# Moving 64 small SBUF copies of transposed e rows from GpSimd's queue to ScalarE's, with two row tiles in turn

## Chip, cores, metric

One core of one Trainium2 chip. The metric is the device time of one execution in microseconds (us). Most executions agree within 0.3%, some are up to 1% longer, so differences of a few us need several runs of both kernels on the same chip. PE is TensorE (PEld its weight loads), DVE is VectorE, ACT is ScalarE, POOL is GpSimd, SP is SyncE. A name with q (ACTq) is the engine's sequencer, which issues DMAs.

## The reference

The program computes a transformer block for one token (attention over a cache of 32 heads x 8192 rows x 192, then an MLP) and the gradients of its inputs, the large ones being dK and dV, each as large as its cache. The second half of the kernel forms them.

```
p = softmax(scores);  o = p @ v                        # scores = q @ k^T * Dh**-0.5
dV[j, :]  = p[j] * do                                  # outer product: one row of e times do
dS[j]     = p[j] * (V[j] . do - c);  dK[j, :] = dS[j] * q
```

## The kernel before

For each of 64 steps (half a head each) PE forms dV from `er_b`, a tile that holds rows of the transposed e at partitions 0, 32, 64 and 96. A row tile `er_t` is made once in four steps by a PE transpose and a ScalarE copy; `load_er` then moves 32 of its rows (8 KB) into `er_b` by a DMA. `load_er` and all stores are issued by GpSimd, whose instruction order the program doesn't pin. In the views, KB and VX are tiles in which dV and dK are formed and from which they are stored; VB takes V loads.

```python
ORDER = {mybir.EngineType.PE, mybir.EngineType.DVE, mybir.EngineType.Activation, mybir.EngineType.SP}
erp = ctx.enter_context(tc.tile_pool(name="erp", bufs=1))
...
def e_rows(t, pool=psS, tag="s"):
    ...                                            # PE transpose of E_all into ps
    er = erp.tile([P, P], BF16, name="er_t")
    A_.copy(out=er[0 : 2 * J, :], in_=ps[0 : 2 * J, :])
    return er
...
ctx.enter_context(tc.manual_schedule(engines=ORDER))
...
er_b = [bst.tile([P, R8, P], BF16, name=f"er_b{k}") for k in range(2)]
def load_er(s):
    er = er_b[s % 2]
    h, t = ht(s)
    r0 = (h % 2) * J + t * JH
    nc.gpsimd.dma_start(out=er[0:P:32, :, :], in_=er_t[0][r0 : r0 + JH, :])
    return er
...
V_.memset(er_b[1], 0.0)
er_l = {0: load_er(0), 1: load_er(1)}
...
def store(dst, s, src, lo=0, hi=JH):
    h, t = ht(s)
    nc.gpsimd.dma_start(out=dst[h][:, t * JH + lo : t * JH + hi, :], in_=src[:, lo:hi, :])
...
# weight gradients: two of the chunks are held back on purpose
keep = lambda w=cur["w"]: nc.gpsimd.dma_start(out=dst[:, :, lo : lo + CW], in_=w)
if dst is dwm_v and n in (GX - 2, GX - 1):
    kept.append(keep)
else:
    keep()
...
def dv_gen():
    for s in range(NS):
        dV, er, doh = out_b(2 * s), er_l.pop(s), do_of(ht(s)[0])
        for n, g in enumerate((0, 2, 4, 6, 1, 3, 5, 7)):
            dv_groups(dV, er, doh, (g,))           # PE matmuls with er, ScalarE copies into dV
            if n == 7:
                if s % 4 == 2 and s + 2 < NS:
                    er_t[0] = e_rows(TL - s // 4 - 1)
                if s + 2 < NS:
                    er_l[s + 2] = load_er(s + 2)
                store(dV_hd, s, dV, JQ if s == 0 else 0, JH)
...
# main loop, step s: dots on PE, dK on DVE, store of dK, next V load on SyncE
    if s in (NS - 4, NS - 3):
        kept.pop(0)()                              # the held-back stores go out in the last steps
```

Of the kernel before, what the change touches and what calls it, by code (L numbers as in the profile page):

```python
# [8 lines left out]
FP32 = mybir.dt.float32  # L9
# [11 lines left out]
def kernel(  # L21
# [26 lines left out]
    nc = tc.nc  # L48
    P = 128
    D = A_x.shape[-1]  # L50
    _, HQ, S, DH = A_k_cache.shape
# [4 lines left out]
    JH = J // 2  # L56
    JQ = J // 4
    TS = 16
    ND = D // P
# [13 lines left out]
    V_, A_, T_ = nc.vector, nc.scalar, nc.tensor  # L73
# [10 lines left out]

    dram = ctx.enter_context(tc.tile_pool(name="dram", bufs=1, space=bass.MemoryType.DRAM))
    ORDER = {mybir.EngineType.PE, mybir.EngineType.DVE, mybir.EngineType.Activation, mybir.EngineType.SP}
    erp = ctx.enter_context(tc.tile_pool(name="erp", bufs=1))

    A_.preload_act_table_set("natural_log_exp_and_others")
    ident_bf = const.tile([P, P], BF16, name="ident_bf")  # L90
# [63 lines left out]
    def layernorm(x, name):  # L154
        res = []
        for _ in g_layernorm(x, name, res):
            pass
        return res[0]
# [94 lines left out]
    n0, r0 = layernorm(x_c, "ln0")  # L253
# [83 lines left out]
    def e_rows(t, pool=psS, tag="s"):  # L337
        ps = pool.tile([P, P], BF16, name="er_ps", tag=tag)
        T_.transpose(out=ps[0 : 2 * J, :], in_=E_all[:, 2 * t : 2 * t + 2, :].rearrange("p h j -> p (h j)"), identity=ident_bf)
# [4 lines that stand above are left out]
    with tc.tile_pool(name="vs", bufs=3) as vsp, tc.tile_pool(name="ft", bufs=2) as ft, \  # L344
# [185 lines left out]
        if True:  # L530
# [224 lines left out]
            er_t = [e_rows(TL, psB, "b")]  # L755
# [8 lines left out]
    bst = ctx.enter_context(tc.tile_pool(name="bst", bufs=1))  # L764
# [83 lines left out]
    def load_er(s):  # L848

        er = er_b[s % 2]  # L850
        h, t = ht(s)
        r0 = (h % 2) * J + t * JH
        nc.gpsimd.dma_start(out=er[0:P:32, :, :], in_=er_t[0][r0 : r0 + JH, :])  # L853
        return er

    def ht(s):

        return H1 - s // 2, (1 - s % 2 if s < 4 else s % 2)
# [147 lines left out]
    nc.sync.dma_start(out=dao_bc, in_=dao_d.to_broadcast([P, D]))  # L1006
    V_.tensor_scalar(out=dx1, in0=e4, scalar1=vv[:, 0:1], scalar2=-1.0, op0=ALU.add, op1=ALU.mult)
    V_.tensor_tensor(out=dao, in0=dx1, in1=ga, op=ALU.mult)
    cpp, cp1 = bst.tile([P, DH], FP32, name="dq_junk")[:, 0 : HQ * ND].rearrange("p (h k) -> p h k", k=ND), bst.tile([P, HQ], FP32, name="cp1")
    V_.tensor_tensor(out=cpp, in0=AO.rearrange("p k h -> p h k"), in1=dao[:, None, :].to_broadcast([P, HQ, ND]), op=ALU.mult)  # L1010
    V_.reduce_sum(out=cp1, in_=cpp, axis=AX.X)
    V_.memset(er_b[1], 0.0)
    er_l = {0: load_er(0), 1: load_er(1)}
    dq_x = bst.tile([P, 12], FP32, name="dq_x")
    V_.memset(dha, 0.0)
# [268 lines left out]
# [4 lines that stand above are left out]
                dv_groups(dV, er, doh, (g,))  # L1288
# [6 lines that stand above are left out]
                elif n == 3 and s == 0:  # L1295
                    store(dV_hd, s, dV, 0, JQ)
                yield
# [26 lines left out]
    for s in range(NS):  # L1324
        h, t = ht(s)
# [3 lines left out]
        if s == 1:  # L1329
# [5 lines left out]
            out=dS4,  # L1335
# [77 lines left out]
```

## Time and profile before

| | before |
|---|---|
| time, median of 3 runs (range) | 1409.15 us (1407.72 to 1409.96) |
| bytes moved | 570.88 MB, mean 406 GB/s |
| DMA rate 700 to 1300 us | 416 GB/s, mean DMA share 1.01 |
| PE waits for er_b, ScalarE waits for er_t | 11.1 us, 10.5 us |

First the page's DMA queues (packets, MB, share of the 16 engines): q1 is SyncE's, q0 GpSimd's, q10 ScalarE's.

```profile
q1 hardware_dynamic: 55372, 342.48, 59.9%
q0 software_dynamic: 26736, 226.48, 38.8%
q10 hardware_dynamic: 20, 0.00, 0.0%
```

Then windows of the second half (start:end and length in us; busy us of PE, PEld, DVE, ACT and POOL; granted TensorE clock; DMA share, which is the busy share of the core's 16 DMA engines; GB/s). The first one is the start of the loop, where the transfers aren't saturated; after 586 us they are.

```profile
555.00:586.00 31.00, 26.98 (x393) 20.24 (x392) 26.49 (x75) 22.23 (x40) 12.08 (x20) 0.74 0.81 264
586.00:700.00 114.00, 83.25 (x752) 49.29 (x750) 79.96 (x107) 64.29 (x101) 19.38 (x33) 0.69 1.00 402
700.00:1300.00 600.00, 446.17 (x3664) 258.46 (x3662) 415.92 (x591) 356.09 (x519) 94.37 (x160) 0.65 1.01 416
```

Last, the timeline where the dV work begins (start, length, engine, line, idle before it in brackets). The move for this first step went out long before, at 555.7 us, and PE starts without a wait.

```profile
568.46 0.82 PE L1050 MATMUL dv_ps<-do_r,er_b 32*128 32x192 bf16 x8
568.57 0.17 ACT L1004 COPY h<-h_ps 128x5 f32<-128x5 f32 x1 [0.60 <-PE h_ps L907]
```

### The profile page before, as it was taken

The page shows a single profiled execution, that of the slowest core. Times are in us where ns is not written, and L with a number is a line of the kernel's source. Part 1 is how long each engine was busy: PE and PEld are TensorE (multiplying, and loading weights), DVE is VectorE, ACT ScalarE, POOL GpSimd, SP SyncE. Part 2 cuts the span into 40 slices and gives each one's busy share as a digit, 9 for nine tenths or more (in the row PEclk, how much of TensorE's full clock was granted, in tenths as well). Part 3 has the DMA queues.
Part 4 walks back from the last instruction along what each step waited for, and adds up shares of the span by engine and source line. Part 5 has one row for each costly group of instructions (what it writes and reads, how often), then busy time and mean ns, then how long its engine had stood idle before and what let it go on. Part 6 is the DMA issues. An engine that isn't in the chain of part 4 may idle for free. (4 is left out here: it accounts for less than half of the span.)

```text
span 1407.8 us, 30000 instructions
## 1 busy us (share of the span) xinstructions
PE 1121.3 (80%) x12543; PEld 745.1 (53%) x12543; DVE 1109.3 (79%) x1380; ACT 878.3 (62%) x1934; POOL 153.0 (11%) x270
## 2 busy tenths in 40 slices
PE   3999999899999998777867768787876777777783
PEld 1677777677777767444434434444443444444441
DVE  4999999999999998785767767676766766866783
ACT  0777777777777773655665656566654665655653
POOL 0000000000000001211111111111111111111111
PEclk9999999999999998876766675657576656665755
DMA  9999999999999998899999999999999999999998
GB/s 375 404 419 421 418 415 417 407 417 416 420 410 420 411 417 314 314 366 425 425 422 422 417 420 426 420 415 402 423 419 408 387 417 417 426 418 403 394 382 348
DMA packets 82264, 570.88 MB, mean 406 GB/s; under 512 B 12464, under 2 KB 31232, under 8 KB 42192
## 3 DMA queue, kind: packets, MB, share of 16 engines
q1 hardware_dynamic: 55372, 342.48, 59.9%
q0 software_dynamic: 26736, 226.48, 38.8%
q8 instruction: 98, 1.61, 0.4%
q14 instruction: 38, 0.31, 0.1%
q10 hardware_dynamic: 20, 0.00, 0.0%
HBM read 341.64 MB, written 225.91 MB: 403 GB/s over the span
## 5 line engine op out<-in xcount | busy, mean ns | idle before, releaser
L1051 ACT CAST KB<-dv_ps 128x768 bf16<-128x768 f32 x416 | 314.9, 804 | 186.8 <-PE dv_ps L1050 180.4
L1039 PE MATMUL dot_ps<-w3p,ident_bf 128*128 128x256 bf16 x1536 | 324.1, 372 | 84.5 <-DVE w3p L1030 84.2
L376 ACT ACTIVATE vs<-VB,Ef 128x192 bf16<-128x192 bf16 x840 | 303.2, 443 | 0.0
L1039 PEld LDWEIGHTS <-ident_bf 128*128 128x128 bf16 x1536 | 176.1, 125 | 190.4 <-issue 140.5
L1050 PE MATMUL dv_ps<-do_r,er_b 32*128 32x192 bf16 x2048 | 202.7, 307 | 68.6 <-ACT KB L1051 46.1
L307 DVE TENSOR_TENSOR prod<-KB,q_ring 128x6144 bf16<-128x6144 bf16 x62 | 207.9, 3353 | 16.4 <-DMA KB<-in_A_k_cache_dram 10.9
L1055 DVE TENSOR_TENSOR KB<-q_ring,dS 128x3072 bf16<-128x3072 bf16 x100 | 175.2, 1753 | 48.8 <-DMA out_dram<-KB 40.9
L391 PE MATMUL mp<-vs,KB 128*128 128x193 bf16 x1920 | 184.8, 248 | 0.0
L1050 PEld LDWEIGHTS <-er_b 32*128 32x128 bf16 x2048 | 85.8, 105 | 175.0 <-issue 159.2
L391 PEld LDWEIGHTS <-KB 128*128 128x128 bf16 x1920 | 164.9, 98 | 18.6 <-issue 6.5
L1030 DVE TENSOR_TENSOR w3p<-VB,do_r 128x3072 bf16<-128x3072 bf16 x96 | 168.1, 1751 | 0.0
L318 PE MATMUL dot_ps<-prod,ident_bf 128*128 128x512 bf16 x372 | 96.2, 397 | 44.8 <-DVE prod L312 44.7
L322 DVE TENSOR_REDUCE dP<-dot_ps 128x32 f32<-128x512 f32 x64 | 44.2, 690 | 101.5 <-PE dot_ps L1039 101.5
L369 DVE TENSOR_TENSOR vs<-VB,E 128x1728 bf16<-128x1728 bf16 x120 | 123.6, 1050 | 0.0
L1051 ACT CAST VX<-dv_ps 128x768 bf16<-128x768 f32 x96 | 73.1, 807 | 63.8 <-PE dv_ps L1050 60.6
L312 DVE TENSOR_TENSOR prod<-prod 128x3072 bf16<-128x3072 bf16 x62 | 108.7, 1754 | 1.0
L874 ACT COPY wT<-wT_ps 128x1024 bf16<-128x1024 bf16 x84 | 81.0, 964 | 42.1 <-PE wT_ps L873 41.7
L396 PE MATMUL mp<-vs,KB 128*64 128x193 bf16 x1920 | 103.8, 251 | 0.0
L853 POOL DMA_DIRECT2D er_b<-er_t x64 | 40.5, 633 | 571.6 <-PE dv_ps L1050 288.8
L396 PEld LDWEIGHTS <-KB 128*64 128x64 bf16 x1920 | 77.3, 110 | 19.2 <-issue 19.1
L356 ACT ACTIVATE E<-S_h,negm 128x256 bf16<-128x256 f32 x30 | 15.2, 508 | 107.5 <-DVE negm L553 107.5
L318 PEld LDWEIGHTS <-ident_bf 128*128 128x128 bf16 x372 | 37.7, 106 | 83.2 <-issue 55.8
(350 smaller groups left out, 1154.0 us busy)
## 6 DMA issues: line engine op xcount, KB each, us to landing
VB<-in_A_v_cache_dram SPq DMA_DIRECT2D x108, 1536.0 KB, 12.2
out_dram<-KB POOLq DMA_DIRECT2D x100, 1536.0 KB, 16.9
KB<-in_A_k_cache_dram SPq DMA_DIRECT2D x63, 1536.0 KB, 12.0
out_dram<-VX POOLq DMA_DIRECT2D x25, 1536.0 KB, 17.2
KB<-in_A_v_cache_dram SPq DMA_DIRECT2D x15, 1536.0 KB, 15.8
wo_st<-in_A_wo_dram SPq DMA_DIRECT2D x30, 480.0 KB, 11.8
w_st<-in_A_wq_dram SPq DMA_DIRECT2D x12, 960.0 KB, 11.8
out_dram<-wo_st POOLq DMA_DIRECT2D x16, 480.0 KB, 18.9
```

The lines of the kernel that those rows point to most:

```text
L307: V_.tensor_tensor(out=prod, in0=src, in1=vec[:, None, :].to_broadcast([P, JH, DH]), op=ALU.mult)
L312: V_.tensor_tensor(out=prod[:, :, 0:w], in0=prod[:, :, 0:w], in1=prod[:, :, w : 2 * w], op=ALU.add)
L318: T_.matmul(ps, lhsT=ident_bf, rhs=prod[:, :, k : k + TS], start=(k == 0), stop=(k == w - TS))
L369: V_.tensor_tensor(out=vs[:, 0:n, 0:DH].rearrange("p j (a b) -> p j a b", b=4), in0=v[:, v0 : v0 + n, :].rearrange("p j (a b) -> p j a b", ...
L376: A_.activation(out=vs[:, k, 0:DH], in_=v[:, v0 + k, :], func=ACT.Copy, scale=Ef[:, j0 + k : j0 + k + 1])
L391: T_.matmul(mp[:, 0:MW], lhsT=kb[:, j0 + k, 0:P], rhs=vs[:, k, 0:MW], start=(q == 0 and k == 0), stop=(z and k == JQ - 1), skip_group_chec ...
L396: T_.matmul(mp[p0 : p0 + 64, MO : MO + MW], lhsT=kb[:, j0 + k, P:DH], rhs=vs[:, k, 0:MW], start=False, stop=(z and k >= JQ - 2), skip_grou ...
L1030: V_.tensor_tensor(out=pq[:, q], in0=v_l[s][:, q * JQ : (q + 1) * JQ, :], in1=do_of(ht(s)[0])[:, None, :].to_broadcast([P, JQ, DH]), op=AL ...
L1039: T_.matmul(ps[:, q * JQ : (q + 1) * JQ, :], lhsT=ident_bf, rhs=pq[:, q, :, k : k + TS], start=(k == 0), stop=(k == DH - TS), skip_group_c ...
L1050: T_.matmul(ps[:, b, k * DH : (k + 1) * DH], lhsT=er[p0 : p0 + 32, 2 * m + k, :], rhs=doh[p0 : p0 + 32, :], start=True, stop=True)
L1051: A_.copy(out=dV4[:, 2 * q : 2 * q + 2, m * PW : (m + 1) * PW], in_=ps[:, :, 0:PW])
L1055: V_.tensor_tensor(out=dK[:, lo:hi, :].rearrange("p j (a b) -> p j a b", b=4), in0=qh.rearrange("p (a b) -> p a b", b=4)[:, None, :, :].to ...
```

## The change

The intent: the small moves no longer stand in GpSimd's queue between stores of 1.5 MB, and with two `er_t` tiles ScalarE need not wait for an earlier move before it writes the next rows. The small scratch `cp1` shares a tile to make room.

```diff
-    erp = ctx.enter_context(tc.tile_pool(name="erp", bufs=1))
+    erp = ctx.enter_context(tc.tile_pool(name="erp", bufs=2))
...
-        nc.gpsimd.dma_start(out=er[0:P:32, :, :], in_=er_t[0][r0 : r0 + JH, :])
+        A_.dma_start(out=er[0:P:32, :, :], in_=er_t[0][r0 : r0 + JH, :])
...
-    cpp, cp1 = bst.tile([P, DH], FP32, name="dq_junk")[:, 0 : HQ * ND].rearrange("p (h k) -> p h k", k=ND), bst.tile([P, HQ], FP32, name="cp1")
+    cpj = bst.tile([P, DH], FP32, name="dq_junk")
+    cpp, cp1 = cpj[:, 0 : HQ * ND].rearrange("p (h k) -> p h k", k=ND), cpj[:, HQ * ND : HQ * (ND + 1)]
```

## The prediction

> **What bounds the kernel now.** The change touches only the second half of the program, from about 555 us on: 64 row-tile steps, each of which loads half a V head, forms dV and dK in SBUF and stores them. I read the slices first.
>
> ```profile
> DMA  9999999999999998899999999999999999999998
> GB/s 375 404 419 421 418 415 417 407 417 416 420 410 420 411 417 314 314 366 425 425 422 422 417 420 426 420 415 402 423 419 408 387 417 417 426 418 403 394 382 348
> ```
>
> From slice 18 on the DMA engines are in their top digit and move 420 to 426 GB/s wherever nothing disturbs them. PE, DVE and ACT are at 60 to 80% there and the granted clock swings between 0.5 and 1.0, so no engine is full. The second half is a transfer-bound loop with some slack on every engine. Time can be won in it only where the transfers run dry or run slow.
>
> What the small moves do is in the view of the tile er_b and in the table of waits:
>
> ```profile
> L853 POOL DMA_DIRECT2D er_b<-er_t x64: 620/632/650, 555.7 to 1375.1; - x64
> DMA to landing us min/median/max: 3.6/9.5/18.2
> ...
> PE dv_ps L1050 <- DMA er_b<-er_t: 11.1, 5, 4.4
> ...
> ACT er_t L341 <- DMA er_b<-er_t: 10.5, 4, 4.9
> ...
> PE bc_t L1111 <- ACT er_t L341: 8.5, 2, 5.3
> ```
>
> An 8 KB move takes 9.5 us (median) to land, up to 18.2, because it shares GpSimd's queue with 1.5 MB stores. Two waits come of it: five times PE waits for er_b (11.1 us in all), and four times ScalarE waits before it overwrites the only er_t, because an earlier move still reads it (10.5 us); PE then waits for ScalarE. The timeline shows the longest of the four, and the windows what it does to the transfers:
>
> ```profile
> 1073.15 0.64 POOL L853 DMA_DIRECT2D er_b<-er_t  x1 [10.73 <-PE q_bc L1377]
> ...
> 1085.53 1.75 DVE L1030 TENSOR_TENSOR w3p<-VB,do_r 128x3072 bf16<-128x3072 bf16 x1
> 1090.49 0.27 ACT L341 COPY er_t<-er_ps 128x128 bf16<-128x128 bf16 x1 [4.89 <-DMA er_b<-er_t]
> ...
> 1091.05 0.63 POOL L853 DMA_DIRECT2D er_b<-er_t  x1 [14.12 <-ACT er_t L341]
> 1091.68 1.08 POOL L1282 DMA_DIRECT2D out_dram<-KB  x2
> ...
> 1084.00:1088.00 4.00, 1.50 (x21) 0.84 (x18) 2.71 (x3) 1.38 (x2) 0.00 (x0) 1.00 1.02 421
> 1088.00:1092.00 4.00, 1.12 (x9) 0.66 (x10) 0.00 (x0) 1.50 (x4) 0.95 (x2) 0.75 0.67 280
> 1092.00:1096.00 4.00, 3.45 (x20) 1.72 (x19) 1.82 (x2) 2.69 (x4) 0.77 (x2) 0.50 0.89 366
> ```
>
> The move issued at 1073.15 lands only about 1090.4. Until then ScalarE stands still, the next move waits for er_t, and a finished dV tile waits behind that move in GpSimd's in-order queue. The DMA share (last column but one) falls to 0.67 and 0.89: 4 us x (0.33 + 0.11) = 1.8 us of transfer time lost. This is the one clear hole in the steady part.
>
> **What the Trainium skill says.** "DMA: Bandwidth & Descriptors", section "Queues, rings and completion order": each DMA engine takes turns, packet by packet, between the queues that have work for it. A move in ScalarE's own queue should then wait for about one packet of the others, not for queued stores. The before trace agrees as far as it goes: a small store on SyncE's queue, issued at 568.0, was followed at 570.3 by the load that needs it, so it landed in at most 2.3 us, against 9.5 us behind the stores. The section "Issuing engines are not separate DMA queues" of that page says that all transfers run on the same 16 engines and another issuer saves only issue time; so no bandwidth is to be won. "Perfetto Trace Analysis", section "DMA Instruction — HWDGE", says that the two hardware issuers lock one descriptor generator in turn. In the trace SyncE's V loads take 327 ns to issue and up to about 1.3 us in the second half when close behind another, so a lock held long is not seen; ScalarE's own two issues at the start take 0.55 and 0.27 us. The first page's section on the semaphore increment of 16 says a transfer is split by its slowest dimension: a destination of 4 rows uses 4 engines, the lowest-numbered on a hardware queue, a rotating four on GpSimd's. The trace has no engine numbers, so it cannot agree or disagree.
>
> **The change part by part.**
>
> Removed from GpSimd: 64 issues x 0.632 us = 40 us. GpSimd is 11% busy and mostly waits, and a dV store stood behind such an issue for only 0.2 to 0.9 us while its ScalarE copies were ending anyway. Worth about 0.
>
> Added to ScalarE: 64 issues of 0.3 to 0.55 us, 19 to 35 us in its sequencer. Its data path is 60% busy in this half (7.9 of 13.2 us). In three of four moves the wait is for PE reads that the last dV copy has waited for too, so the issue runs beside that 0.8 us copy. In 15 moves the issue waits for the fresh er_t copy: a bubble of about 0.5 us, 7 us in all, on an engine that is not the bound. About 0.
>
> Two er_t tiles: the copy no longer waits for moves, so the 10.5 us on ScalarE and 8.5 us on PE go. What counts of it is transfer time: 1.8 us in the hole above, 4 x 0.12 = 0.5 us at 976 to 980 us where the share reads 0.88, and the slow recovery after both: 26 us at 363 GB/s instead of 424 is 26 x (1 - 363/424) = 3.7 us (it includes the 1.8), the same sum for 397 GB/s at 976 to 1002 is 1.7 us. Not all of that comes from the wait, since weight chunks with 1.5 KB rows pass there too. I take -4.
>
> The 11.1 us of PE waits on er_b go as well. In those stretches (e.g. 898 to 911 us) the DMA share stays at 1.00, so they are worth about 0, by choice.
>
> The start moves the wrong way. GpSimd, which is outside the pinned order, issued the first move at 555.7, long before it was needed. In the built program both first moves stand on ScalarE after the copy of h, so they go out at about 568 to 568.6. PE's first dV matmuls ran at 568.46. With about 2.3 us to land they start near 570.5, and PE was packed from there to 577. Transfers are not yet saturated there (share 0.63 to 0.87), so most of it counts: +1.5 to +2.
>
> Four fixed engines: 2 KB for each of four engines a move. At 406/16 = 25.4 GB/s an engine that is 81 ns, x64 = 5.2 us on these four, where a rotating four gives each of the 16 engines 1.3 us. If the four were the slowest in a bound loop, this would cost 4 us; I count +1 (an estimate).
>
> The cp1 scratch in a shared tile only makes room; reuse comes much later. 0.
>
> Sum: -4 + 1.75 + 1 = about -1.5 us, so 1409.15 becomes 1407.5.
>
> **The rivals.** (a) ScalarE is held up by its issues: the generator is locked by SyncE, or the move's completion counter is shared with a load not yet landed. In the built program the counter a move uses was last used about three steps (some 40 us) earlier, mostly by a V load; those land in 12 us, 30.5 at most, so it should rarely bind. If ScalarE lost 3 us on a third of the moves, some 60 us of stalls partly show: 1415 to 1425. (b) The waits on PE and ScalarE count in full, because delayed stores hold the loop later (DVE waits 40.9 us for KB stores and 9.2 for VX): 11 + 10 us minus the start gives 1390 to 1397. Against it stands the DMA share of 1.00 in nearly all windows. (c) Everything is hidden and only the start shows: 1410 to 1412. (d) PE's granted clock falls when PE waits less; it would eat a gain, not add a loss.
>
> **Range and chances.** The mechanism bounds the gain at some 1% and my costs at 6 us; a shift of step order can add 3 us either way, with repeats spread by 2 us. Range 1399 to 1414. Faster by over 2% (below 1381) needs more than all waits named: 0.02. Slower by over 2% needs rival (a) at its worst: 0.02.
>
> **What would show it.** Right: er_b landing at 2 to 4 us median; the waits PE dv_ps <- er_b and ACT er_t <- er_b gone, except one PE wait of 1.5 to 3 us at the first dV; no hole with a share below 0.9 between 640 and 1340 us; ScalarE issues near 0.4 us. The same GB/s plateau shows that the loop was transfer-bound. Wrong: ScalarE waiting for DMA at the moves, issues over 1 us, a plateau below 420 GB/s (the four engines), or a second half shorter by over 10 us at the same bytes, which would mean that the small waits were on the path after all.

## The result, and the profile after

The changed kernel took 1414.1 us (median of 4 runs, 1412.3 to 1417.06) against 1408.47 of the kernel before beside it: ratio 1.0041, 95% interval 1.0020 to 1.0061. It is slower by about 6 us, inside 2%, and just outside the range of the prediction. A ratio here is the mean time of one kernel's fast runs over that of the other's fast runs of the same rounds, so not quite the ratio of the medians. Five more rounds later gave 1.0027. The mean of both is 1.0034, about +4.8 us on 1409. The profiled execution (span 1415.3 us) is the slowest of its four, so single times late in its trace are late by some us in any case.

In the changed kernel the code after line 1009 stands one line lower (L1050 became L1051, L1282 became L1283). The moves are now on ScalarE's sequencer. From its view of line 853 (ns min/median/max, first and last start), and from the table of waits of PE:

```profile
L853 ACTq DMA_DIRECT2D er_b<-er_t x64: 542/543/645, 567.3 to 1388.0; - x64
...
PE dv_ps L1051 <- DMA er_b<-er_t: 5.8, 5, 3.5
```

An issue takes 0.54 us. ScalarE's wait for er_t is gone, PE's wait for er_b is halved, and of the 5.8 us left one wait has 3.5. It is the first dV matmul:

```profile
567.27 0.16 ACT L1004 COPY h<-h_ps 128x5 f32<-128x5 f32 x1 [0.61 <-PE h_ps L907]
567.33 1.30 ACTq L853 DMA_DIRECT2D er_b<-er_t  x2
570.73 0.82 PE L1051 MATMUL dv_ps<-do_r,er_b 32*128 32x192 bf16 x8 [3.50 <-DMA er_b<-er_t]
```

ScalarE's order is pinned, so the first move stands behind the copy of h and goes out at 567.3 instead of 555.7. Everything ahead of it had run 1.3 us earlier than in the trace of before; even so PE starts 2.3 us later. The moves themselves did not become quick. The view gives no landing for them, but the trace keeps every DMA packet with its queue and time, and a packet of these moves is one row or one completion. On ScalarE's queue the last packet of a move ends 8.7 us (median; 1.4 to 12.9) after the start of its issue, 8.8 us in the repeat after_again. On e10 below, where the view has a landing, this count gives 8.4 us and the view 9.0. So a move lands about as late as the 9.5 us before; what went is the long end, 18.2 us.

In the steady part an issue runs beside a copy of the same engine, as here:

```profile
750.72 0.80 ACT L1052 CAST KB<-dv_ps 128x768 bf16<-128x768 f32 x1 [1.03 <-PE dv_ps L1051]
750.73 0.54 ACTq L853 DMA_DIRECT2D er_b<-er_t  x1
```

The windows, the counterpart of those before:

```profile
555.00:586.00 31.00, 25.27 (x368) 18.76 (x365) 22.79 (x62) 19.89 (x35) 7.91 (x13) 0.64 0.73 241
586.00:700.00 114.00, 81.65 (x761) 49.23 (x759) 79.76 (x114) 66.35 (x104) 15.84 (x27) 0.73 0.99 396
700.00:1300.00 600.00, 441.44 (x3623) 254.56 (x3624) 415.36 (x590) 353.26 (x513) 63.83 (x112) 0.66 1.01 414
```

The start moves less (241 GB/s instead of 264), and the 600 us of the steady part are not faster (414 against 416), although the hole at 1088 us that I wanted to close is closed: from 1080 to 1106 us the kernel before moves 363 GB/s, the changed one 422:

```profile
1080.00:1106.00 26.00, 23.56 (x167) 12.29 (x166) 18.43 (x28) 15.91 (x23) 2.12 (x4) 0.50 1.01 422
```

So something gives it back. In part it is other holes in the same stretch. In windows of 4 us from 640 to 1340 us, the kernel before has a share below 0.9 at 976 and at 1088 to 1096; the changed one has it at 1020 to 1028 (0.75 and 0.87) and at 1312 (0.70), its repeat at 1312 (0.73). Added up over these windows, a share below 1 costs 4.5 us of transfer time before, and 5.5 and 4.4 us in the two traces of the changed kernel. In the hole at 1020 DVE waits 7.6 us until a store has left a KB tile, and GpSimd has no store to issue for 15.2 us; in the one at 1312 GpSimd waits 8.7 us for a weight tile (stg, the first of the two held-back stores below).

More is seen near the end. 1370 to 1390 us, first the kernel before, then the changed one:

```profile
1370.00:1390.00 20.00, 14.58 (x118) 7.30 (x116) 14.24 (x12) 14.71 (x20) 3.93 (x7) 0.67 1.00 398
```

```profile
1370.00:1390.00 20.00, 17.29 (x112) 8.63 (x111) 15.38 (x13) 11.86 (x17) 2.00 (x4) 0.50 0.71 293
```

The DMA engines run dry there: 20 us x (1 - 293/398) = 5.3 us of transfer time in this trace (the repeat, after_again, has 363 GB/s there; more on this at e15). What differs is the order of the stores. The last V load, and the two held-back weight stores (960 KB each, the rows with stg and w_st), in the kernel before:

```profile
1341.61 0.33 SPq L302 DMA_DIRECT2D VB<-in_A_v_cache_dram  x1
1367.10 0.89 POOL L1134 DMA_DIRECT2D out_dram<-stg  x1 [0.19 <-issue]
1377.07 0.88 POOL L1134 DMA_DIRECT2D out_dram<-w_st  x1
```

and in the changed kernel:

```profile
1313.32 0.87 POOL L1135 DMA_DIRECT2D out_dram<-stg  x1 [8.70 <-DVE stg L1131]
1348.79 0.87 POOL L1135 DMA_DIRECT2D out_dram<-w_st  x1 [4.05 <-DVE w_st L1131]
1354.36 0.33 SPq L302 DMA_DIRECT2D VB<-in_A_v_cache_dram  x1
```

The program holds these two stores back for the last steps, when nothing is loaded any more. GpSimd's order isn't pinned, and with the moves gone from it the build puts both stores before the last V load, into the part that is bound by transfers. I compared the built programs: with the moves on GpSimd (kernel before, two tiles alone) all 170 stores stand in one and the same order; with the moves on ScalarE the dK and dV stores are also swapped through most of the loop. The traces agree: 44 of the 170 places hold a store of another tile in the changed kernel, none with two tiles alone. The change in a few lines thus is also a new order of all stores. I had compared the built programs for ScalarE before I predicted, but had not read GpSimd's order.

### The profile page after: what moved, and what is told of

Same layout as the page of the kernel before. It is cut to its first block, busy times and chain, and to the rows that moved or that the text cites. A ratio compares the mean times of both kernels' runs of the same rounds, so it can differ in the third digit from the quotient of the medians.

```text
span 1415.3 us, 29991 instructions
## 1 busy us (share of the span) xinstructions
PE 1122.9 (79%) x12543; PEld 744.2 (53%) x12543; DVE 1109.7 (78%) x1380; ACT 879.0 (62%) x1934; POOL 112.1 (8%) x206
## 3 DMA queue, kind: packets, MB, share of 16 engines
q10 hardware_dynamic: 2324, 0.53, 0.2%
## 4 chain that ended last, share of the span: by engine, by line
issue 38%; DVE 24%; DMA 17%; PE 13%; POOL 5%; ACT 2%; POOLq 0%; SPq 0%; ACTq 0%; DVEq 0%
DVE prod L307 9%; DMA KB<-in_A_k_cache_dram 7%; DVE prod L312 5%; DMA out_dram<-VX 4%; POOL out_dram L1283 4%; DMA out_dram<-KB 4%; DVE vs L369 3%; PE dot_ps L1040 3%; PE mp L391 3%; PE dot_ps L318 2%; DVE S_h L322 2%; PE mp L396 1%; DVE w3p L1031 1%; DMA VX<-in_A_v_cache_dram 1%; PE dv_ps L1051 1%
## 5 line engine op out<-in xcount | busy, mean ns | idle before, releaser
L1051 PE MATMUL dv_ps<-do_r,er_b 32*128 32x192 bf16 x2048 | 201.5, 304 | 71.0 <-ACT KB L1052 51.6
L1056 DVE TENSOR_TENSOR KB<-q_ring,dS 128x3072 bf16<-128x3072 bf16 x100 | 175.2, 1753 | 68.1 <-DMA out_dram<-KB 56.4
L1051 PEld LDWEIGHTS <-er_b 32*128 32x128 bf16 x2048 | 84.0, 104 | 179.2 <-issue 169.1
L1283 POOL DMA_DIRECT2D out_dram<-KB x104 | 56.2, 541 | 498.3 <-DVE KB L1056 219.1
L356 ACT ACTIVATE E<-S_h,negm 128x256 bf16<-128x256 f32 x30 | 15.2, 508 | 107.5 <-DVE negm L553 107.5
```

The source lines that it names most:

```text
L1051: T_.matmul(ps[:, b, k * DH : (k + 1) * DH], lhsT=er[p0 : p0 + 32, 2 * m + k, :], rhs=doh[p0 : p0 + 32, :], start=True, stop=True)
L1056: V_.tensor_tensor(out=dK[:, lo:hi, :].rearrange("p j (a b) -> p j a b", b=4), in0=qh.rearrange("p (a b) -> p a b", b=4)[:, None, :, :].to ...
```

## The experiments

18 runs, three of them repeats ("again"), all correct in their results. "us" is (ratio - 1) x 1409.

| run | edit in short | ratio, 95% interval | us |
|---|---|---|---|
| after_again | the change, repeat | 1.0027 [0.9999, 1.0056] | +3.8 |
| e13_first_two_act | before, only moves 1 and 2 on ScalarE | 1.0031 [1.0001, 1.0061] | +4.4 |
| e1_first_two_pool | change, moves 1 and 2 on GpSimd | 1.0013 [0.9989, 1.0038] | +1.8 |
| e1_again | the same | 0.9999 [0.9968, 1.0029] | -0.1 |
| e14_act_late_one_tile | before, moves 3 to 64 on ScalarE | 1.0003 [0.9975, 1.0031] | +0.4 |
| e3_act_one_tile | change, one er_t tile | 1.0031 [1.0005, 1.0057] | +4.4 |
| e2_pool_two_tiles | before, two er_t tiles | 0.9993 [0.9964, 1.0021] | -1.0 |
| e2_again | the same | 0.9984 [0.9948, 1.0020] | -2.3 |
| e15_store_order | e1, GpSimd's order pinned | 0.9992 [0.9964, 1.0021] | -1.1 |
| e10_act_sixteen_rows | before, useless move on ScalarE, 16 engines x 5 rows | 1.0006 [0.9978, 1.0035] | +0.8 |
| e11_act_eight_rows | same, 4 engines x 8 rows | 1.0010 [0.9976, 1.0045] | +1.4 |
| e12_act_four_halves | same, 4 engines x 20 rows | 1.0025 [0.9992, 1.0058] | +3.5 |
| e4, e5, e6, e7, e8, e9 | heavier useless moves | 1.0069 to 1.0464 | confounded |

The theories: **S**, the late start is the loss; **I**, ScalarE is held up by its issues; **E**, the four DMA engines that serve every move are overloaded; later **O**, the new order of the stores gives the gain back.

### The start: e1, e13, and their complements

e1 takes the late start out of the changed kernel:

```diff
-        A_.dma_start(out=er[0:P:32, :, :], ...)
+        (nc.gpsimd if s < 2 else A_).dma_start(out=er[0:P:32, :, :], ...)
```

> The changed kernel, but the first two of the 64 small moves are issued by GpSimd again, the first of them early as before. Theory S (the late first move is the loss: in the changed kernel's trace PE waits 3.50 us for it at the first dV matmul): 3.5 us come back, 1409 to 1411, near the kernel before. Theory E (62 moves on four fixed DMA engines slow the transfers) or theory I (62 issues of 0.54 us hold ScalarE up): the first moves matter little, 1412 to 1415, still 4 us or more above the kernel before.

1413.79 us against 1411.28, ratio 1.0013. Run again beside the changed kernel:

> The kernel with the first two moves on GpSimd once more. Theory S alone: 3.5 us below the changed kernel and within 1 us of the kernel before. Theories S and E together: 3.5 us below the changed kernel and still 2 to 4 us above the kernel before.

> The changed kernel once more, on the same chip as the next three, to have its loss beside theirs. All theories: 1.002 to 1.006 of the kernel before.

e1 gave 0.9999, the changed kernel 1.0027. Mean of e1: 1.0006; mean of the changed kernel: 1.0034; the difference, 0.28% or 3.9 us, is close to the wait of 3.5 us. In the rounds that had both (after_again, e1_again) the means differ by 4.0 us, with some 2.7 us to either side (my estimate from the scatter of the runs). e13 does the reverse: it puts the late start into the kernel before. (In its trace the fourth and fifth store are swapped too, as in the changed kernel; all others stand as before.)

```diff
-        nc.gpsimd.dma_start(out=er[0:P:32, :, :], ...)
+        (A_ if s < 2 else nc.gpsimd).dma_start(out=er[0:P:32, :, :], ...)
```

> The kernel before with only the first two of the 64 moves on ScalarE's queue, all others as before, one er_t tile. Theory S (the late start is the loss): PE waits about 3.5 us at the first dV matmul, the first move goes out near 568 instead of 556, and the time rises by 3 to 4.5 us, ratio 1.002 to 1.003. Prediction on record for this term: +1.75 us, 1.0012. Rival (the start is made good later by a loop that waits for transfers anyway): within 1 us, 0.9995 to 1.0007.

Ratio 1.0031, +4.4 us. Its timeline shows the same wait:

```profile
568.89 1.30 ACTq L853 DMA_DIRECT2D er_b<-er_t  x2
572.52 0.82 PE L1050 MATMUL dv_ps<-do_r,er_b 32*128 32x192 bf16 x8 [3.73 <-DMA er_b<-er_t]
```

So the 3.6 us from the start of the issue (568.89) to the first use (572.52) reach the end of the program about whole, as far as an interval of 0.1 to 8.6 us can tell. The window from 555 to 586 us offers a reason: e13 moves 227 GB/s there, the kernel before 264; 31 us x 37 GB/s are 1.15 MB, which take 2.8 us at 416 GB/s, and the loop after it is saturated. The other traces agree: with the late start 227 to 245 GB/s in this window (changed kernel twice, e3, e13), with the early one 256 to 279 (the kernel before and all others that have a row of their own in the table). The complement of e13:

> The complement: the kernel before with moves 3 to 64 on ScalarE's queue, the first two on GpSimd's, one er_t tile. If the late start is all that the changed kernel lost and the second tile does nothing once the moves have their own queue: the same as the kernel before within 1.5 us, 0.999 to 1.001, and as e1, with no wait of ScalarE for er_b. If the four fixed engines cost the 1 to 2 us that e11 and e12 leave room for and nothing pays for it: 1.0007 to 1.0015.

Ratio 1.0003. Start (+4.4) and rest (+0.4) add up to the change (+4.8). Theory S holds.

### The two tiles: e2 and e3

e2 is the kernel before with `bufs=2` and the cp1 lines of the change; e3 is the changed kernel with `bufs=1`.

> The changed kernel with all 64 moves on GpSimd: the two row tiles alone. If the waits of ScalarE for er_t were worth what I predicted (4 us, without the costs of the queue): 1404 to 1406. If they were hidden: 1408 to 1409, as before. In either case the whole loss belongs to the queue.

> The two er_t tiles alone (moves stay on GpSimd's queue), a repeat because the interval of the first run, 0.9964 to 1.0021, still holds the -4 us that I predicted for it. Prediction as on record: ratio 0.9972. Rival: the holes that the wait made are only moved, ratio 0.999 to 1.001.

> The changed kernel with one row tile: the queue alone. The moves now land sooner, so the copy of a new er_t should hardly wait for the old one: as the changed kernel, 1413 to 1415 (all theories). If the second tile still carries a gain, it is slower, 1416 to 1419.

e2 gave 0.9993 and 0.9984, mean -1.6 us. ScalarE's waits for er_t are gone in both runs, but PE's waits for er_b rose from 11.1 us to 17.7 and 14.7. Two runs with half-widths of 0.29% and 0.36% leave about 0.23% for their mean, so the -4 us that I predicted isn't excluded, nor is nothing. e3 equals the changed kernel and has no wait for er_t either: once the moves have their own queue, one tile is enough, and the second does nothing that these runs can see.

### ScalarE's issues: e4 and e10

e4 adds to the changed kernel, per step, a useless 4 KB move into DRAM on ScalarE:

```diff
+        A_.dma_start(out=junk_d[:, 0:P], in_=ident_bf[0:16, :])
```

> The changed kernel with a second, useless 4 KB move of 16 rows (one 256-byte row for each DMA engine, into a scratch in DRAM) issued by ScalarE behind each of the 64: it doubles the issue time on ScalarE (another 64 x 0.5 us) and adds next to nothing to the transfers. Theory I: the part of the loss that comes of the issues doubles, 1417 to 1421. Theories S and E: no change beyond 2 us, 1413 to 1416.

Ratio 1.0075 [1.0053, 1.0097], +10.6 us, or 1421.8 us: just above the range of theory I, and clear of that of S and E. But it is no clean test: two issues together (1.1 us) outlast the 0.8 us copy that hides one, and the writes of 256 B go to the same place in DRAM each time. Why a second move costs this much stays open. e10 adds one issue per step to the kernel before, whose moves stay on GpSimd:

```diff
+        if s >= 2:
+            A_.dma_start(out=AO.rearrange("p k h -> p (k h)")[0:P:8, 0:40].rearrange("p (r e) -> p r e", e=8), in_=ident_f[0:80, 0:8])
```

> Its control: the same 80 rows with 16 outer rows on ScalarE's queue, 5 rows for each of 16 engines. It pays the same issues (62 x 0.54 us on ScalarE). Theory I: above the kernel before by 2 to 4 us, as the four-row run. Theory E: a quarter of the four-row run's loss. Neither: 1408 to 1411.

Ratio 1.0006. 62 issues of 0.54 us, 34 us in ScalarE's sequencer, cost nothing measurable, and ScalarE waited for none of these moves. The interval, -3.1 to +4.9 us, still holds the 2 to 4 us of theory I; With the real issues and no late start (e1 twice, e14) the loss is 0.7 us in the mean, so a cost of the issues can be there only with a gain beside it.

### The four engines: e5 to e9, e11, e12

A move with 4 outer rows (the slowest dimension of its target, here partitions 0, 32, 64 and 96) should use 4 DMA engines, as the prediction cites. The trace has no engine numbers, but its packet counts agree: the changed kernel has

```profile
q0 software_dynamic: 24688, 225.93, 38.1%
q10 hardware_dynamic: 2324, 0.53, 0.2%
```

so a move on ScalarE's queue is (2324 - 20)/64 = 36 packets: 32 rows of 256 B and 4 completions. e10's moves of 80 rows in 16 outer rows are (5972 - 20)/62 = 96 packets: 80 rows and 16 completions. To amplify the load I added useless moves with 4 outer rows, and controls with 16: e5 and e6 on SyncE into DRAM after each V load (`out=junk_d..., in_=ident_bf`, 128 rows of 256 B), e7 and e8 on SyncE within SBUF, e9 on ScalarE (as e10, but `[0:P:32, :]`, 20 rows for each of four engines).

> The kernel before (moves on GpSimd, one tile) with a useless move of 32 KB on SyncE's queue behind each of the 60 V loads of the loop: 128 rows of 256 bytes, shaped with 4 outer rows. If the split by the slowest dimension puts it on four fixed DMA engines, each of these gets 60 x 32 x 18 ns = 35 us more work and every load and store waits for the slowest of them. Theory E: 1425 to 1445. Without a tie to four engines (spread over 16): 60 x 8 x 18 ns = 9 us on each, 1412 to 1420, and the same time as the run with 16 rows.

> The control of the run with 4 outer rows: the same 128 rows of 256 bytes, shaped with 16 outer rows, so that every engine gets 8 of them. Theory E: 9 us of work on each engine and an issue of the same kind, 1412 to 1420, below the four-row run by 10 us or more. If four engines do not matter: as the four-row run within 3 us.

> The kernel before with a useless move inside SBUF on SyncE's queue behind each of the 60 V loads: 80 rows of 32 bytes into a tile that is dead by then, with the 4 outer rows of the small moves, so 20 rows for each of four engines (the small moves have 8). Theory E with the 34 to 43 ns a row that the two runs with rows into DRAM lost: 60 x 20 x 34 to 43 ns = 41 to 52 us more than before if rows inside SBUF cost the same; 15 to 25 us if they cost their 14 to 18 ns; 0 to 5 us if four engines do not matter inside SBUF.

> Its control: the same 80 rows of 32 bytes with 16 outer rows, 5 for each of 16 engines. Theory E: a quarter of what the four-row run loses against the kernel before. If four engines do not matter: the same as the four-row run.

> The kernel before (moves on GpSimd, one tile) with the useless move of 80 rows of 32 bytes, 4 outer rows, on ScalarE's queue where the changed kernel issues its moves, for 62 steps. In the two runs with this move on SyncE's queue the trace shows SyncE waiting 507 and 420 us for the landing of the one before, behind V loads, so their losses may be those of late loads and not of four engines. On ScalarE's own queue the move lands within a few us and nothing waits for it. Theory E at 35 to 40 ns a row: 62 x 20 rows on four engines, 1450 to 1460. E at the 9 ns that a 32-byte row takes: 1413 to 1421. If neither rows nor issues matter: 1408 to 1411.

e5 1.0464, e6 1.0148, e7 1.0337, e8 1.0069, e9 1.0266. The form with four rows is always the dearer one, which looked like theory E. But e7, e8 and e9 wrote the same bytes in every step, so each move had to wait for the one before it, and behind it the loads or ScalarE's work: e7 shows 506.9 us of such waits in SyncE's queue, e8 420.1, and e9 among others these on ScalarE (total us, times, longest):

```profile
ACT q_ring L1380 <- DMA AO<-ident_f: 49.4, 9, 8.2
ACT wT L876 <- DMA AO<-ident_f: 22.4, 5, 8.3
```

(e9's profiled run was also slow.) e5 and e6 write into one place in DRAM again and again too, and their traces show the same waits on SyncE, 514.9 and 466.6 us. These five don't tell load from wait. e11 and e12 remove the wait: the target alternates between two halves of the tile.

```diff
+            A_.dma_start(out=AO.rearrange("p k h -> p (k h)")[0:P:32, 80 * (s % 2) : 80 * (s % 2) + 80].rearrange("p (r e) -> p r e", e=10), in_=ident_f[0:32, 0:10])
```

(e12: `e=4` and 80 rows.)

> The kernel before plus, per step from the third on, one useless move on ScalarE's queue with the row count of the real one: 32 rows of 40 B into partitions 0, 32, 64, 96 (8 rows each, so the same four engines 62 times), alternating between two halves of its target so that it doesn't wait for the one before it. Theory E (the four fixed engines cost time at the size of the real move): +2 to +8 us over the kernel before, ratio 1.0015 to 1.006. Rival N (eight rows for each of four engines are hidden, and what the changed kernel lost is its late start): within 1.5 us, ratio 0.999 to 1.001. Both: 36 packets a move in the ScalarE queue's count, landing 8 to 13 us, no wait of ScalarE for an earlier move.

> As the run before it, but 80 rows of 16 B (20 for each of the four engines). It is the amplified form of the four-engine load without the wait for its own predecessor that spoiled e9. Theory E: a loss in proportion to rows, 2.5 times that of eight rows, +5 to +20 us, ratio 1.0035 to 1.014. Rival N: e9 lost by its waits alone, so this one is within 2 us, ratio 0.9985 to 1.0015. If ScalarE still waits for an earlier move, the run tells nothing and I say so.

e11: 1.0010; e12: 1.0025, with one wait of 0.2 us on ScalarE for such a move. So most of e9's 37 us went with its own waits (the rows of e12 are also half as long, 16 B for 32). With 2.5 times the rows of the real move the loss is 3.5 us, with the row count of the real move 1.4 us, and both intervals hold zero. The two agree with a small cost in proportion to the rows and with none. My +1 us for this term is neither confirmed nor refuted. The working behind it was low: from the packet records the changed kernel's packets on ScalarE's queue took 39.4 us, so 9.8 us on each of four engines, not 5.2.

### The order of the stores: e15

> As e1 (the changed kernel with the first two moves left on GpSimd's queue), with one more line: GpSimd is pinned to the program's order from the loop on. In the build this puts its store queue back into exactly the order of the kernel before (no difference in 170 stores), where e1 and the changed kernel store the two last held-back weight tiles (960 KB each) some 40 to 60 us earlier and swap dK and dV stores. Theory O (the gain of the own queue is given back because the store order changed: the last V load is issued about 6 us later, 1348 instead of 1342, and the tail runs dry at 1370 to 1390): last V load at 1336 to 1343, no slice below 350 GB/s at 1370 to 1390, time 3 to 6 us below the kernel before, ratio 0.996 to 0.998. Rival Z (the waits for the small moves never were worth anything, the order doesn't matter): the hole may move, time as e1, ratio 0.9995 to 1.001. Rival E (the four fixed engines eat it): the hole is gone but the plateau from 700 to 1300 is below 414 GB/s, ratio near 1.

e1 with one line more, after the first two moves:

```diff
     er_l = {0: load_er(0), 1: load_er(1)}
+    ctx.enter_context(tc.manual_schedule(engines=ORDER | {mybir.EngineType.Pool}))
```

In the build all 170 stores are back in the order of the kernel before. Ratio 0.9992, -1.1 us. Rival E expected a plateau below 414 GB/s here; in the trace it is 418, as in both traces of e2, whose moves go through GpSimd's queue:

```profile
700.00:1300.00 600.00, 439.26 (x3687) 253.67 (x3687) 418.10 (x598) 358.67 (x522) 64.02 (x114) 0.68 1.01 418
```

The trace (span 1401.7 us, the fastest of its runs) shows the held-back stores and the last load where the program wants them:

```profile
1337.12 0.33 SPq L302 DMA_DIRECT2D VB<-in_A_v_cache_dram  x1
1362.17 0.87 POOL L1136 DMA_DIRECT2D out_dram<-stg  x1
1374.22 0.87 POOL L1136 DMA_DIRECT2D out_dram<-w_st  x1
```

and the rate in the 20 us of the hole:

```profile
1370.00:1390.00 20.00, 9.84 (x88) 4.95 (x83) 11.86 (x10) 12.41 (x17) 4.07 (x7) 0.67 0.93 367
```

One dip is left (331 in 1370 to 1380 us), against my expectation of none below 350. A single trace could be chance, so here are the profiles of all kernels that have a row of their own in the table, by the order of their stores:

| order of stores | profiles | from the issue of the last V load to the end | GB/s in that time | GB/s, 1370 to 1390 us |
|---|---|---|---|---|
| as before | before, e2 (2), e10, e11, e12, e13, e15 | 64.0 to 66.2 us | 358 to 375 | 355 to 399 |
| as in the change | changed (2), e1 (2), e3, e14 | 59.0 to 62.9 us | 337 to 359 | 275 to 309, once 363 |

The new order has less left to move after the last load (some 21.2 MB, against 22.9 to 24.0), and has moved the rest in the bound part before. Over this whole tail it also moves more slowly. At the mean rate of the first row, 364 GB/s, 21.2 MB take 58.3 us; the second row took 61.1 us in the mean. So the dry tail costs about 2.8 us (an estimate), less than the 5.3 us of one window in one trace. Part of that window is the granted clock: it was 0.50 to 0.67 in the five traces with 275 to 309 GB/s and 0.84 in the one with 363. At 0.50 the old order (e13) still has 355, so the order counts as well. DVE's waits for stores, in e15:

```profile
DVE KB L1057 <- DMA out_dram<-KB: 10.4, 6, 4.2
DVE VX L1057 <- DMA out_dram<-VX: 5.8, 3, 3.9
```

In the kernel before these were 40.9 and 9.2 us, in the changed one 56.4 and 16.4, in its repeat 40.6 and 10.7. So the order decides how much is left after the last load: that is shown. That it decides where DVE waits isn't, since the kernel before has the order of e15 and about four times its wait for KB. What the order is worth in time is not settled. I expected 0.996 to 0.998; the interval of e15 holds that and zero, and the difference to e1 and e14 (mean 1.0005) is 1.8 us with an error of more than that. What e15 does suggest is that waits are cheap here: in its trace 34 us of DVE waits and 17 us of waits for er_b and er_t went, for about 1 us (5 at the end of the interval).

No version beats the kernel before beyond its interval; e2 and e15 come nearest, at -1.6 and -1.1 us.

## Why the prediction was wrong

The class (within 2%) was right, the reading of the loop as transfer-bound was right, and the terms that I set to about 0 agree with the runs. The time came out some 6 us too low through two terms.

- **"Two er_t tiles ... I take -4"** is the step that failed. It priced the closing of one hole as transfer time won, and supposed that the rest of the schedule stays. The hole closed, but others opened: from 640 to 1340 us the share below 1 costs 5.5 and 4.4 us in the changed kernel, against 4.5 before, and the 600 us of the plateau move 414 and 415 GB/s against 416. In time, three runs with the moves on ScalarE and no late start (e1 twice, e14) have a mean of 1.0005, about +0.7 us, with an interval of some 0.16% if they are independent (-1.6 to +3.0 us), where my terms -4 and +1 ask for -3 us. Their sum lies outside the interval. Taken alone, -4 isn't refuted: two tiles on GpSimd's queue gained 1.6 us (e2, twice), give or take 3. Why the holes moved is open in part: the order of the stores changed and its dry tail costs an estimated 2.8 us, but e15, which restores the order, gained only 1.1 us, and its interval is 4 us to either side.
- **"A move in ScalarE's own queue should then wait for about one packet of the others"** failed as well, and with it the sign "er_b landing at 2 to 4 us median": 8.7 us. The stores ahead in GpSimd's queue were not most of what makes a move slow. I had set a landing of 2.3 us at 568 us, where the transfers aren't saturated, against a median of 9.5 us where they are; the two moves that e1_again left on GpSimd's queue landed in 4.2 and 4.5 us at the start.
- **"Most of it counts: +1.5 to +2"**: the mechanism and its place were foreseen, the size was half of what came. From issue to use I took 2.3 us; here it was 3.4 us (3.6 in e13), so the wait was 3.5 us (3.7) where I had allowed 1.5 to 3. Measured: +3.9 us (changed kernel less e1) and +4.4 us (e13) for my +1.75. Each has an interval of about 4 us, so it is the trace that shows the term too small.
- **"Four fixed engines: ... +1"** stays open: e11 says 1.4 us, with -3.4 to +6.3 as its interval; the plateau of e15 speaks against a large cost.
- **"Added to ScalarE ... About 0"** agrees with e10. Rival (a), which I feared most, did not come: no issue took over 0.65 us.
- **"The 11.1 us of PE waits on er_b go as well ... worth about 0, by choice"** agrees with e15, which has 4.5 us of them and gains about 1 us with everything else. Rival (b), 12 us or more below, is outside every interval. Rival (d) did not come: the mean granted clock is 0.787 before and 0.788 after.

So 4.15 us (the mean of 3.9 and 4.4) replaces 1.75 for the start, and +0.7 replaces the -3 of the two other terms: 4.85 us, where the change measured +4.8. The parts share runs with the whole, so this sum is a check and no proof. Rival (c), everything hidden and only the start shows, had the right shape with too small a start. Of the other signs, "no hole with a share below 0.9 between 640 and 1340 us" failed (0.75 at 1020, 0.70 at 1312), and issues took 0.54 us, not 0.4. "A plateau below 420 GB/s" could not tell anything: the kernel before has 416.

## What to carry to other kernels

A DMA moved from an engine whose order is free to one whose order is pinned takes on that engine's place in the program: look at the first use of what it brings, and leave the first transfers where they could go early. Read the order of the engine that loses instructions as closely as that of the one that gains them; if a schedule depends on stores held back by hand, pin the engine that issues them. In a loop bound by transfers, neither a wait nor a hole in the trace is a gain until the bytes after it also come earlier: add up the lost share over the whole loop, before and after.

## What the Trainium skill lacked or had wrong

- "DMA: Bandwidth & Descriptors", section "Queues, rings and completion order": each engine takes turns between queues by packets, a packet of that page being some 9 to 17 descriptors. I read from it that a small move in its own queue waits for about one packet of the others. e10's move, 5 rows of 32 B and a completion for each engine, took 9.0 us (median, 5.8 to 11.7) to land beside the saturated loop:

```profile
DMA to landing us min/median/max: 5.8/9.0/11.7
```

  In the packet records of the changed kernel 4.1 us (median) pass from the issue to the first row of a move, and 4.5 us from there to its last completion; for the first move, before the transfers saturate, it is 2.4 us and about 0.5. The page has no time for a small transfer with many rows beside full queues.
- The same page, section "Why a DMA increments its semaphore by 16 and not by 1": the counts agree with it (4 completions for a move with 4 outer rows and 16 for 16 on the hardware queues, 16 for each move on GpSimd's). It doesn't say how GpSimd's queue cuts up the data of such a move: by the sizes of the packets that are missing there after the change, 4 packets of 2 KB and 12 of 32 B, where ScalarE's queue has 32 rows of 256 B.
- "Perfetto Trace Analysis", section "DMA Instruction — HWDGE", speaks of one descriptor generator locked in turn by the two issuers, and gives no times. What the runs show: 0.54 us for an issue on ScalarE (median; 0.65 at most), beside a running copy, and no measurable loss from 62 of them (1.0006).
- No page that I read says that taking DMAs off an engine with a free order makes the build reorder that engine's other DMAs; here it moved two stores of 960 KB by about 54 and 28 us between the two traces.
